# A fused attention and SiLU kernel: v's second cast and products moved ahead of q's last copies, batch 2's loads moved back, and the positions of the next two stages rewritten with them

## The chip, the cores and the metric

The kernel runs on one core of a Trainium2 chip. TensorE multiplies matrices into PSUM. VectorE and ScalarE read PSUM and write SBUF, [...]and SyncE (SP) issues most of the DMA transfers. The engines run beside each other, each in the order of its own list of instructions, and wait for one another through semaphores.

The metric is the device time of one execution, in microseconds (us). Before the change the median of four runs is 266.94 us (266.63 to 267.75).

## The reference

```python
def _attn_ref(q, k, v):                     # (8, 8, 576, 64): batch, head, row, d
    q_s = softmax(q, over d)
    k_s = softmax(k, over the 576 rows)
    kv = einsum('bhsd,bhse->bhde', k_s, v)
    return einsum('bhsd,bhde->bhse', q_s, kv)

def _moe_ref(x, w_in, w_out):               # x: (4608, 512)
    h = x @ w_in                            # (4608, 2048)
    return (h * sigmoid(h)) @ w_out         # (4608, 512)
```

The attention's output, heads side by side, is x. Inputs and output are float32 in memory; the products run on bfloat16.

## The kernel before

**Batches and stages.** There are eight batches (576 rows each) and nine stages t (512 rows of x each, except that stage 0 takes the whole first batch). Stage t computes the first layer for its rows (`mm1`, or `product1` where it uses Strassen's seven products for eight), SiLU (`act1`, `silu1`), and the second layer of the rows before it (`mm2` for stage 0, `product` and `after` for the others, the latter adding up the Strassen products and storing). The attention of batch b is prepared during stage b - 1, and `xt` makes the rows of x for stage t at the end of stage t - 1.

**One batch of attention**, in two halves `cc` of two head pairs each:

- `load` brings q, k and v from memory (`qt`, `kt`, `vt`; q and v have one buffer, k two).
- `exp` (ScalarE) makes `eq` and `ek`.
- `qsum` (VectorE) sums the rows of `eq`, `qnorm` scales them.
- `tr` and `trc` transpose `eq` on TensorE and copy the result to `qT`, each half in two pieces of 5 and 4 blocks; `tr_dma` lets the DMA engines do it instead.
- `vcast` casts v to `vaug`, which has a column of ones beside each head. `kv` (72 small products for a batch, 36 for a half) gives the score matrix and, from the column of ones, the divisor. `kvcopy` takes the reciprocal and scales to `kvn`.
- `xt` multiplies `kvn` and `qT`, `xtcopy` copies the result from PSUM to `XT`.

**PSUM.** `kv`, `tr`, `xt`, `mm1` and `product1` share a ring of six buffers; a product waits until the buffer that it is given has been copied or passed through SiLU. Two more buffers serve the second layer.

**Order.** The start (lines 598 to 646) is written out by hand for batch 0. `START['t']` says which engine makes each of the four transposed copies (0 VectorE, 1 GpSimd, 2 ScalarE), `START['h']` how many idle products `heat` puts at four places to keep TensorE busy. After that, everything is recorded with `put(t, position, function, ...)`, sorted by position and emitted: the tables `PLAN[t]`, `TXAT` and `TWAT` hold the positions. Within a stage the position counts TensorE's steps. So each engine's list follows from numbers, and an instruction only waits for what it needs and for what stands before it on its own engine.

The entries of `PLAN[t]` that matter here, for the batch prepared in stage t: `ex` positions of the four `exp` (q, q, k, k), `qs` and `qn` of `qsum` and `qnorm`, `vs` of `vcast`, `ks` and `kc` of `kv` and `kvcopy`, `ke` the engine of its scaling, `tp`, `tt`, `tc`, `te` of the transposes and their copies, `ox` and `oc` of `xt` and `xtcopy`, `lq`, `lk`, `lv` of the loads of the batch after. For the layers: `order` of the Strassen products (group, product), `sl` of the SiLUs, `add`, `act`, `s1` of the sums and SiLUs of those products, `xs` and `xe` of the four sums of XT (S1 to S4) that the products need, `pa`, `pb` and `pae` of `presum` (sums of the SiLU results), `y` and `ya` of the second layer's products and of `after`. `TXAT` and `TWAT` place the sums of the weights (`vsum` for the first layer, `wsum` for the second).

**Weights.** They come through GpSimd's queue, cast on the way, in the order of `WORDER`: w10 to w13, w20, q of batch 1, w21, w22, k, the first half of v, w23, the second half of v. `load_first` brings q, k and v of batch 2 on SP. It first lets VectorE write one element of the q buffer (line 663), so that the load waits for that point.

Of the kernel before, what the change touches and what calls it, by code (L numbers as in the profile page):

```python
# [18 lines left out]
PLAN = {  # L19
    0: {'y': [31.0, 33.0, 33.0, 33.5, 34.0, 34.5, 35.0, 35.5, 36.5, 37.0, 39.5, 41.5, 42.5, 44.5, 46.0, 47.0], 'ex': [31.7, 34.3, 39.3, 39.4], 'qs': [33, 35.5], 'qn': [37.0, 39.5], 'vs': [40.0, 37.5, 42.0, 43.5], 'ks': [45.0, 45.8], 'kc': [45.51, 46.31], 'lq': 39.0, 'tp': 39.0, 'ox': [47.1, 47.7], 'oc': [47.11, 47.71], 've': [1, 1, 1, 2], 'order': [(1, 0), (2, 0), (3, 1), (0, 1), (3, 0), (0, 0), (1, 1), (6, 0), (2, 1), (6, 1), (4, 0), (5, 0), (7, 1), (11, 0), (5, 1), (8, 1), (4, 1), (7, 0), (8, 0), (9, 0), (10, 1), (11, 1), (9, 1), (14, 0), (13, 1), (12, 1), (14, 1), (15, 0), (12, 0), (10, 0), (15, 1), (13, 0)], 'ke': [0, 1], 'oe': [0, 1], 'qe': [0, 0], 'pad': 16, 'th': [0, 1], 'tt': [43.5, 37.4, 42.0, 39.9], 'tc': [43.51, 41.5, 43.01, 41.0], 'te': [0, 2, 0, 2]},  # L20
    1: {'ex': [16.7, 16.72, 22.24, 23.26], 'qs': [17.65, 17.9], 'qn': [19.1, 18.1], 'vs': [22.5, 20.5], 'ks': [23.5, 25.5], 'kc': [26.01, 27.01], 'lq': 15.0, 'lk': 7.5, 'lv': 21.5, 'tp': 18.1, 'ox': [28.5, 29.0], 'oc': [29.01, 29.01], 've': [2, 2], 'pa': [10.9, 13.0, 15.0], 'pae': [0, 0, 0], 'ke': [0, 0], 'oe': [0, 2], 'std': 4, 'order': [], 'add': {}, 'act': {}, 's1': {0: 0, 1: 1, 2: 1, 3: 1}, 'sl': [0.5, 1.5, 3.5, 6.0, 6.0, 7.5, 7.0, 9.0, 9.0, 9.5, 11.5, 11.0, 14.5, 13.0, 15.0, 15.0], 'xs': [3.3, -24.9, -4.5, -2.5], 'xe': [1, 1, 0, 1], 'pad': 14, 'qe': [1, 0], 'th': [0], 'tt': [22.5, 21.1], 'tc': [23.51, 24.6], 'te': [2, 2]},
    2: {'std': 2, 'order': [(3, 1), (3, 6), (2, 1), (2, 6), (3, 7), (3, 5), (3, 2), (2, 7), (3, 4), (2, 2), (2, 5), (2, 4), (2, 3), (3, 3)], 'y': [-14.0, -12.5, -12.3, -12.25, -11.5, -11.0, -10.0, -9.5, -9.0, -5.0, -3.0, -2.5, -1.5, -0.5], 'ex': [0.2, -0.79, -3.6, -4.09], 'qs': [4.9, 3.4], 'qn': [11.91, 4.41], 'vs': [-3.08, 13.9], 'ks': [19.4, 20.9], 'kc': [19.91, 20.91], 'lq': 22.5, 'lk': 20.0, 'lv': 30.91, 'tp': 21.4, 'ox': [21.4, 21.4], 'oc': [21.41, 21.41], 'sl': [4.5, 8.5, 3.0, 5.5, 9.0, 9.0, 12.0, 10.5], 'add': {(3, 6): 9.55, (3, 3): 22.02, (3, 1): 9.55, (3, 5): 13.55, (3, 4): 17.55, (2, 2): 20.02, (3, 2): 20.02, (3, 7): 13.55, (2, 1): 10.55}, 'act': {(3, 5): 15.02, (3, 3): 22.02, (2, 5): 18.02, (3, 4): 19.02, (2, 4): 21.55, (2, 3): 22.02, (2, 7): 18.02, (3, 7): 14.55, (3, 2): 15.55, (2, 1): 12.02, (3, 6): 11.55}, 's1': {2: 0, 3: 0}, 'xs': [1.6, 2.6, 7.6, 4.6], 'pa': [18.95, 22.95, 20.95], 'ya': {2: -8.0, 6: -12.2, 3: 1.5, 5: -4.55}, 'm1': [1, 0], 'pb': [-14.9, -14.3, -12.39, -15.0, -5.0], 'xe': [0, 0, 0, 0], 'pae': [1, 0, 1], 'pbe': [0, 0, 0, 0, 0], 've': [1, 2], 'ke': [1, 0], 'oe': [1, 0], 'qe': [1, 1]},
}
# [4 lines left out]
PLAN[9] = {'y': [0, 1, 2, 3, 4, 5, 6, 7, 8, 9, 10, 11, 12, 13], 'ya': {}, 'm1': [0, 0], 'pb': [-0.201, -0.2, -0.2, 1.9, 2.9], 'pbe': [0, 0, 0, 0, 0]}  # L28
TXAT = [(0, (0, -5.5, 0, 0)), (0, (0, 20.0, 1, 1)), (1, (1, -28.5, 0, 0)), (1, (1, -6.0, 1, 1)), (2, (1, 2.0, 0, 0)), (2, (0, 12.5, 1, 0)), (3, (2, -23.5, 0, 0)), (3, (2, -30.5, 1, 1))]
TWAT = [(0, 26.0, 0), (1, 2.0, 0), (1, 2.0, 1), (1, 7.0, 1), (1, 12.5, 1), (0, 55.5, 0), (0, 32.0, 1), (0, 40.0, 0)]  # L30
WORDER = ['w10', 'w11', 'w12', 'w13', 'w20', 'q', 'w21', 'w22', 'k', 'v0', 'w23', 'v1']
# [3 lines left out]
STD = 0  # L35
START = {'qn': (0, 0), 'h': [4, 3, 2, 1], 'v': 0, 't': (0, 0, 0, 2), 'x': 1, 'o': 0, 'w': 4}

@with_exitstack
def kernel(
# [80 lines left out]
    def vcast(b, cc, eng, gs=(0, 2)):  # L120
        if gs[0] == gs[1]:
            return
        gs = slice(2 * cc + gs[0], 2 * cc + gs[1])
        o = vaug.rearrange("p j (g e) -> p j g e", e=E1)[:, :, gs, 0:D]
        i = st[b]["vt"][:, gs, :].rearrange("p g (j d) -> p j g d", d=D)
        if eng is nc.scalar:
            eng.copy(out=o, in_=i)
        else:
            eng.tensor_copy(o, i)
# [38 lines left out]
    def trc(b, cc, js, eng=nc.vector):  # L168
        t = st[b]["qtps", cc, js[0]]
        o, i = qt_tile(b)[:, cc, slice(*js), :], t[:, 0:js[1] - js[0], :]  # L170
        if eng is nc.scalar:
            eng.copy(out=o, in_=i)
        else:
            eng.tensor_copy(o, i)
# [16 lines left out]
    def kvcopy(b, cc, act=0):  # L191
        rzs = []
        for r in range(2):
            rz = ap.tile([128, 1], FP32, name="rz", bufs=4)
            nc.vector.reciprocal(out=rz, in_=st[b]["kvps", cc][r][:, D:E1])
            rzs.append(rz)
        for r in range(2):
            kp, rz = st[b]["kvps", cc][r], rzs[r]
            y = kvn[b % 3][:, cc, r, :]
            if act == 1 or act == 2 and r:  # L200
                nc.scalar.activation(out=y, in_=kp[:, 0:D], func=ACT.Copy, scale=rz[:, 0:1])
            else:
                nc.vector.tensor_scalar_mul(out=y, in0=kp[:, 0:D], scalar1=rz[:, 0:1])
# [29 lines left out]
    def xtcopy(t, cc, dve=0):  # L233
        for i, (off, size) in enumerate(part[t]):
            o1 = XO.pop((t, cc, i), None)
            if o1 is None:
                continue
            for g in range(2):
                x = XT[t][:, 2 * cc + g, off:off + size]
                if g < dve:  # L240
                    nc.vector.tensor_copy(x, o1[g][:, 0:size])  # L241
                else:
                    nc.scalar.copy(out=x, in_=o1[g][:, 0:size])  # L243
# [151 lines left out]
    ENG = (nc.vector, nc.gpsimd, nc.scalar)  # L395
# [198 lines left out]
    def heat(n):  # L594
        for _ in range(n):
            nc.tensor.matmul(out=wps, lhsT=warm[:, 0:128], rhs=warm, start=True, stop=True)

    HALF = ((0, 5), (5, J))
# [24 lines left out]
    for js in HALF:  # L623
        tr(0, 1, js)
    kvcopy(0, 0)
    for i, js in enumerate(HALF):
        trc(0, 1, js, ENG[SB["t"][2 + i]])
    heat(SB["h"][2])
    if SB["x"]:
        xt(0, 0)  # L630
    vcast(0, 1, nc.scalar, (0, 1))
    vcast(0, 1, ENG[SB["v"]], (1, 2))
    heat(SB["h"][3])
    kv(0, 1)
    if SB["x"]:
        xtcopy(0, 0, 1)
    kvcopy(0, 1, 2)
    if not SB["x"]:
        xt(0, 0)
        xtcopy(0, 0, 1)  # L640
    xt(0, 1)
# [143 lines left out]
```

The softmax here doesn't subtract the row's maximum and nothing guards it: scores larger than these inputs give would overflow.

## Time and profile before

| what | value |
|---|---|
| median of four runs | 266.94 us |
| the profiled execution | 267.75 us |
| its span on the core | 265.9 us |
| TensorE busy | 253.3 us |
| ScalarE busy | 188.0 us |
| VectorE busy | 196.2 us |
| GpSimd busy | 148.4 us |
| first product of `mm1` | 15.62 us |
| last product of stage 0's first layer | 31.3 us |
| first product of stage 1's first layer | 48.09 us |
| first product of stage 2's first layer | 75.24 us |
| first product of stage 3's first layer | 91.06 us |
| v's second half, batch 0: issued, landed | 3.34, 12.54 us |
| q, k, v of batch 2: issued on SP | 38.95, 39.42, 44.70 us |
| v of batch 3: issued, landed | 70.52, 78.02 us |

[...] The span runs from the first instruction to the last; the time holds 1.85 us more around it. Busy times of the other engines add up to much less than the span, and an idle stretch of theirs matters only if TensorE waits for what comes behind it.

### The profile page before, as it was taken

How to read it: one execution, taken by the hardware profiler on the slowest of the kernel's cores; microseconds unless marked ns; L12 is line 12 of the kernel's file. 1: busy time of each engine (PE TensorE's matmuls, PEld its weight loads, DVE VectorE, ACT ScalarE, POOL GpSimd, SP SyncE). 2: the span in 40 equal slices, each digit the busy share in tenths (PEclk: the TensorE clock that was granted, in tenths of full speed). 3: DMA queues.
4: the chain of work that ended last, by engine and by line, in shares of the span. 5: the costliest groups of instructions: out<-in, count | busy, mean ns of one | idle time of the engine just before them, and what ended most of it. 6: DMA issues, size and time to landing. Idle time of an engine off the chain costs nothing.

```text
span 265.9 us, 6578 instructions
## 1 busy us (share of the span) xinstructions
PE 253.3 (95%) x2690; PEld 200.4 (75%) x2695; DVE 196.2 (74%) x335; ACT 188.0 (71%) x326; POOL 148.4 (56%) x94
## 2 busy tenths in 40 slices
PE   8789999999999899999999989999999999999993
PEld 3468645457857688888888778888888887888882
DVE  2935185677887999689977598779877678898842
ACT  5689963869987899689968498879784557454300
POOL 2555047831128579757976785759676546603500
PEclk9999999999999999999999999999999999999999
DMA  7999999960998936757665756391621102110334
GB/s 253 324 206 270 231 333 396 359 202 8 222 300 237 297 121 198 149 160 282 208 130 151 293 184 128 85 346 48 141 73 41 39 22 59 42 39 12 76 75 118
DMA packets 39565, 45.61 MB, mean 172 GB/s; under 512 B 15216, under 2 KB 27504, under 8 KB 39536
## 3 DMA queue, kind: packets, MB, share of 16 engines
q1 hardware_dynamic: 34240, 37.33, 47.2%
q0 software_dynamic: 5136, 7.73, 13.2%
q8 instruction: 21, 0.34, 0.6%
q10 hardware_dynamic: 160, 0.13, 0.2%
q14 instruction: 8, 0.07, 0.1%
HBM read 36.70 MB, written 9.44 MB: 174 GB/s over the span
## 4 chain that ended last, share of the span: by engine, by line
PE 65%; DVE 14%; DMA 9%; ACT 3%; POOL 3%; issue 3%; SPq 1%; DVEq 0%; ACTq 0%; POOLq 0%
PE ops L450 24%; PE hps L349 19%; PE hps L256 13%; DMA kt<-in_k_dram 5%; PE ops L535 5%; DVE u L367 4%; DVE zq L137 3%; DMA qT<-eq 2%; PE kvps L183 2%; DMA qt<-in_q_dram 1%; PE o L225 1%; ACT eq L118 1%; SPq L524 1%; POOL eq L145 1%; DVE eq L145 1%
## 5 line engine op out<-in xcount | busy, mean ns | idle before, releaser
L450 PEld LDWEIGHTS <-GT 128*128 128x128 bf16 x512 | 49.6, 98 | 8.2 <-issue 2.0
L349 PEld LDWEIGHTS <-TX 128*128 128x128 bf16 x416 | 40.1, 98 | 8.6 <-issue 2.5
L349 PE MATMUL hps<-XS,TX 128*128 128x256 bf16 x312 | 43.3, 273 | 1.8 <-DVE XS L306 1.1
L367 DVE SCALAR_TENSOR_TENSOR u<-hps,s 128x512 f32<-128x512 f32 x52 | 35.4, 683 | 11.3 <-PE hps L349 9.2
L367 DVE SCALAR_TENSOR_TENSOR u<-hps,u 128x512 f32<-128x512 f32 x52 | 35.7, 687 | 10.6 <-PE hps L349 8.2
L450 PEld LDWEIGHTS <-SW 128*128 128x128 bf16 x384 | 37.2, 98 | 4.9 <-DVE SW L407 0.4
L391 ACT ACTIVATE GT<-u 128x512 bf16<-128x512 f32 x52 | 32.1, 631 | 7.5 <-DVE u L367 7.5
L256 PE MATMUL hps<-XT,W 128*128 128x320 bf16 (+3 forms) x223 | 35.4, 318 | 0.5 <-ACT XT L243 0.3
L349 PEld LDWEIGHTS <-W 128*128 128x128 bf16 x312 | 30.4, 98 | 4.4 <-issue 0.4
L450 PE MATMUL ops<-W,GT 128*128 128x256 bf16 x256 | 31.7, 273 | 1.4 <-ACT s L480 1.4
L450 PE MATMUL ops<-TW,SW 128*128 128x256 bf16 x256 | 32.9, 273 | 0.0
L450 PE MATMUL ops<-TW,GT 128*128 128x256 bf16 x256 | 32.6, 273 | 0.1
L256 PEld LDWEIGHTS <-W 128*128 128x128 bf16 x224 | 21.8, 98 | 13.3 <-issue 1.2
L137 DVE TENSOR_REDUCE zq<-eq 128x18 f32<-128x1152 bf16 x16 | 21.5, 1341 | 13.4 <-ACT eq L118 13.4
L349 PE MATMUL hps<-XT,W 128*128 128x256 bf16 x208 | 30.4, 273 | 0.4 <-DVE XT L241 0.4
L405 POOL TENSOR_TENSOR SW<-GT 128x1024 bf16<-128x1024 bf16 x7 | 14.9, 2128 | 27.9 <-ACT GT L391 17.4
L145 POOL TENSOR_TENSOR eq<-eq,rzq 128x1152 bf16<-128x1152 bf16 x11 | 23.6, 2151 | 10.8 <-DVE rzq L138 10.6
L411 POOL TENSOR_TENSOR SW<-GT,SW 128x1024 bf16<-128x1024 bf16 x11 | 23.6, 2146 | 9.1 <-DVE SW L407 9.1
L286 ACT ACTIVATE GT<-hps 128x192 bf16<-128x192 f32 (+4 forms) x72 | 25.3, 417 | 4.3 <-PE hps L256 2.9
L409 POOL TENSOR_TENSOR GT<-GT 128x1024 bf16<-128x1024 bf16 x12 | 25.5, 2128 | 0.1
L118 ACT ACTIVATE ek<-kt 128x1152 bf16<-128x1152 f32 x16 | 18.3, 1157 | 9.7 <-DMA kt<-in_k_dram 9.3
L391 ACT ACTIVATE GT<-s 128x512 bf16<-128x512 f32 x26 | 16.4, 632 | 10.1 <-DVE s L367 10.1
(81 smaller groups left out, 397.3 us busy)
## 6 DMA issues: line engine op xcount, KB each, us to landing
qt<-in_q_dram SPq DMA_DIRECT2D x6, 1152.0 KB, 5.7
kt<-in_k_dram SPq DMA_DIRECT2D x6, 1152.0 KB, 6.8
vt<-in_v_dram SPq DMA_DIRECT2D x6, 1152.0 KB, 8.2
out_dram<-u SPq DMA_DIRECT2D x34, 64.0 KB, 3.1
W<-in_moe_w_in_dram POOLq DMA_DIRECT2D x4, 512.0 KB, 8.7
W<-in_moe_w_out_dram POOLq DMA_DIRECT2D x4, 512.0 KB, 18.9
out_dram<-u SPq DMA_DIRECT2D x14, 128.0 KB, 2.6
qt<-in_q_dram SPq DMA_DIRECT2D x2, 576.0 KB, 4.1
```

Of the source, the lines that this page charges most:

```text
L118: nc.scalar.activation(out=o, in_=jgd(st[b][src], cc)[:, js], func=ACT.Exp)
L137: nc.vector.reduce_sum(out=st[b]["zq"][:, cc, js], in_=e, axis=AX.X)
L145: eng.tensor_tensor(out=e, in0=e, in1=r[:, :, :, None].to_broadcast([128, n, 2, D]), op=ALU.mult)
L256: nc.tensor.matmul(out=hps[:, 0:size], lhsT=W1[:, c, fb * 128:(fb + 1) * 128], rhs=XT[t][:, c, off:off + size], start=(c == 0), stop=(c == ...
L286: nc.scalar.activation(out=y, in_=hps[:, h], func=ACT.Silu)
L349: nc.tensor.matmul(out=o[:, f, :], lhsT=l(c, 2 * g + f), rhs=r(c), start=bool(first and f == 0 and c == 0), stop=(c == HK - 1), skip_group ...
L367: nc.vector.scalar_tensor_tensor(out=out, in0=o, scalar=1.0, in1=x, op0=ALU.mult, op1=ALU.add)
L391: nc.scalar.activation(out=y, in_=MP[t, g, x], func=ACT.Silu)
L405: V.tensor_add(S1[:, f], quad(t, 0, f, 1), quad(t, 1, f, 1))
L409: V.tensor_sub(quad(t, 0, f, 1), quad(t, 0, f, 0), quad(t, 0, f, 1))
L411: V.tensor_sub(S4[:, f], quad(t, 1, f, 0), S2[:, f])
L450: nc.tensor.matmul(out=o, lhsT=l(f), rhs=r(f), start=bool(first and (own or a == 0) and f == 0), stop=(f == HF - 1), skip_group_check=True,)
```

## The change

In the start, both parts of `vcast` for the second half of v, then `kvcopy(0, 0)`, `kv(0, 1)` and its `kvcopy` are emitted ahead of the last two transposed copies (`trc`) and of `xt(0, 0)`; the first of those copies goes from VectorE to ScalarE, and the switch `START['x']` is no longer read. The loads of batch 2 move from position 39.0 to 46.5. The positions of stages 1 and 2 and of the sums of the weights change in many places (of each table only the entries that change are shown, several to a line):

```diff
 PLAN[0]
-'lq': 39.0
+'lq': 46.5
 PLAN[1]
-'ex': [16.7, 16.72, 22.24, 23.26], 'qs': [17.65, 17.9], 'qn': [19.1, 18.1], 'vs': [22.5, 20.5]
+'ex': [15.2, 16.72, 23.24, 25.26], 'qs': [17.65, 20.4], 'qn': [23.1, 20.41], 'vs': [24.0, 17.5]
-'ks': [23.5, 25.5], 'kc': [26.01, 27.01], 'lk': 7.5, 'lv': 21.5, 'tp': 18.1
+'ks': [26.5, 26.5], 'kc': [26.51, 27.01], 'lk': 9.5, 'lv': 23.5, 'tp': 21.1
-'ox': [28.5, 29.0], 'oc': [29.01, 29.01], 'pa': [10.9, 13.0, 15.0], 'pae': [0, 0, 0]
+'ox': [28.5, 28.5], 'oc': [28.51, 29.51], 'pa': [10.9, 12.0, 12.0], 'pae': [0, 1, 0]
-'tt': [22.5, 21.1], 'tc': [23.51, 24.6], 'te': [2, 2]
+'tt': [23.5, 23.1], 'tc': [23.51, 27.61], 'te': [0, 2]
...
 PLAN[2]
-'order': [(3, 1), (3, 6), (2, 1), (2, 6), (3, 7), (3, 5), (3, 2), (2, 7), (3, 4), (2, 2), (2, 5), (2, 4), (2, 3), (3, 3)]
+'order': [(3, 1), (3, 6), (2, 1), (2, 6), (3, 5), (3, 7), (2, 2), (2, 7), (3, 2), (3, 4), (2, 5), (2, 4), (3, 3), (2, 3)]
-'y': [-14.0, -12.5, -12.3, -12.25, -11.5, -11.0, -10.0, -9.5, -9.0, -5.0, -3.0, -2.5, -1.5, -0.5]
+'y': [-14.0, -13.3, -12.5, -12.25, -11.5, -10.0, -9.5, -8.0, -6.0, -5.0, -3.0, -2.5, -1.5, -0.5]
-'ex': [0.2, -0.79, -3.6, -4.09], 'qs': [4.9, 3.4], 'qn': [11.91, 4.41], 'vs': [-3.08, 13.9]
+'ex': [0.2, 2.21, -2.1, -0.09], 'qs': [7.9, 6.9], 'qn': [14.91, 11.41], 'vs': [-2.08, 10.9]
-'ks': [19.4, 20.9], 'kc': [19.91, 20.91], 'lq': 22.5, 'lk': 20.0, 'lv': 30.91, 'tp': 21.4
+'ks': [19.4, 20.4], 'kc': [19.91, 20.41], 'lq': 20.5, 'lk': 19.5, 'lv': 24.91, 'tp': 19.9
-'ox': [21.4, 21.4], 'sl': [4.5, 8.5, 3.0, 5.5, 9.0, 9.0, 12.0, 10.5]
+'ox': [20.9, 20.9], 'sl': [2.5, 8.5, 3.0, 5.5, 10.5, 5.5, 11.5, 10.0]
-'s1': {2: 0, 3: 0}, 'xs': [1.6, 2.6, 7.6, 4.6], 'ke': [1, 0]
+'s1': {2: 0, 3: 1}, 'xs': [2.1, 4.1, 3.1, 6.6], 'ke': [1, 1]
...
-TXAT = [(0, (0, -5.5, 0, 0)), (0, (0, 20.0, 1, 1)), (1, (1, -28.5, 0, 0)), (1, (1, -6.0, 1, 1)), (2, (1, 2.0, 0, 0)), (2, (0, 12.5, 1, 0)), (3, (2, -23.5, 0, 0)), (3, (2, -30.5, 1, 1))]
+TXAT = [(0, (0, -8.0, 0, 0)), (0, (0, 20.5, 1, 1)), (1, (1, -29.0, 0, 1)), (1, (0, 24.5, 1, 0)), (2, (1, 0.5, 0, 0)), (2, (0, 9.0, 1, 0)), (3, (1, 2.0, 0, 0)), (3, (2, -29.5, 1, 1))]
-TWAT = [(0, 26.0, 0), (1, 2.0, 0), (1, 2.0, 1), (1, 7.0, 1), (1, 12.5, 1), (0, 55.5, 0), (0, 32.0, 1), (0, 40.0, 0)]
+TWAT = [(0, 30.0, 0), (0, 32.0, 1), (1, 4.0, 0), (1, 4.5, 1), (1, 13.5, 0), (0, 54.5, 0), (0, 32.5, 1), (1, 13.0, 0)]
...
-START = {'qn': (0, 0), 'h': [4, 3, 2, 1], 'v': 0, 't': (0, 0, 0, 2), 'x': 1, 'o': 0, 'w': 4}
+START = {'qn': (0, 0), 'h': [4, 3, 2, 1], 'v': 0, 't': (0, 0, 2, 2), 'x': 1, 'o': 0, 'w': 4}
...
     for js in HALF:
         tr(0, 1, js)
-    kvcopy(0, 0)
-    for i, js in enumerate(HALF):
-        trc(0, 1, js, ENG[SB["t"][2 + i]])
-    heat(SB["h"][2])
-    if SB["x"]:
-        xt(0, 0)
     vcast(0, 1, nc.scalar, (0, 1))
     vcast(0, 1, ENG[SB["v"]], (1, 2))
+    kvcopy(0, 0)
+    heat(SB["h"][2])
+    kv(0, 1)
+    trc(0, 1, HALF[0], ENG[SB["t"][2]])
+    kvcopy(0, 1, 2)
+    trc(0, 1, HALF[1], ENG[SB["t"][3]])
+    xt(0, 0)
     heat(SB["h"][3])
-    kv(0, 1)
-    if SB["x"]:
-        xtcopy(0, 0, 1)
-    kvcopy(0, 1, 2)
-    if not SB["x"]:
-        xt(0, 0)
-        xtcopy(0, 0, 1)
+    xtcopy(0, 0, 1)
     xt(0, 1)
```

Left out are the smaller shifts of the SiLUs and first sums of stage 1, of the single sums and SiLUs of stage 2 (`add`, `act`), and of `after`. As the lists of the engines come out: q, k and v of batch 2 stand on SP behind the stores of three of stage 0's four blocks of rows; v of batch 3 stands behind three stores of stage 1 instead of ahead of them; of the four exponentials of batch 3 one for k moves behind the copies of XT on ScalarE; on VectorE the four sums of XT in stage 2 stand ahead of batch 3's two row sums; the last product of stage 2 stands behind `xt` of stage 3 on TensorE. From stage 3's products on, the code is the same.

## The prediction

> **What bounds the kernel now.** I read the page first, then a table by stretches cut where TensorE's work changes, then TensorE's list of waits, and last the timelines of the engines in the two stretches that the change rebuilds. The page's line of busy time:
>
> ```profile
> PE 253.3 (95%) x2690; PEld 200.4 (75%) x2695; DVE 196.2 (74%) x335; ACT 188.0 (71%) x326; POOL 148.4 (56%) x94
> ```
>
> The table by stretches (from and to in us; length; busy us of PE, PEld, DVE, ACT, POOL; clock; DMA share; GB/s):
>
> ```profile
> 0.00:15.60 15.60, 12.08 (x139) 5.89 (x140) 10.01 (x23) 9.38 (x12) 7.69 (x17) 1.00 0.95 276
> 15.60:31.30 15.70, 15.70 (x131) 12.54 (x129) 5.80 (x6) 14.59 (x50) 4.93 (x5) 1.00 1.19 240
> 31.30:48.10 16.80, 16.22 (x162) 8.22 (x163) 9.61 (x19) 10.11 (x16) 9.39 (x7) 1.00 1.09 351
> 48.10:60.50 12.40, 12.31 (x64) 6.24 (x64) 8.75 (x9) 9.37 (x18) 6.50 (x3) 1.00 0.75 253
> 60.50:75.20 14.70, 14.63 (x210) 12.23 (x209) 12.04 (x24) 13.20 (x17) 2.12 (x1) 1.00 0.61 143
> 75.20:91.10 15.90, 15.20 (x178) 9.84 (x178) 13.76 (x27) 13.56 (x24) 9.92 (x5) 1.00 0.91 263
> ```
>
> From 15.6 us on TensorE is never idle for long, at full clock: the kernel ends when TensorE's list ends. A microsecond is won only where TensorE waits. Its waits (us in total, times, longest), and on TensorE's timeline (start, length) the largest place that the change can reach:
>
> ```profile
> PE ops L450 <- ACT s L480: 1.4, 1, 1.4
> ...
> PE hps L349 <- DVE XS L306: 1.1, 2, 0.6
> ...
> PE o L225 <- DVE kvn L203: 0.6, 1, 0.6
> ```
>
> ```profile
> 89.33 0.61 PE L349 MATMUL hps<-XS,W 128*128 128x256 bf16 x4
> 89.87 0.74 PE L225 MATMUL o<-qT,kvn 64*64 64x192 bf16 x16
> 91.06 0.60 PE L349 MATMUL hps<-XT,W 128*128 128x256 bf16 x4 [0.45 <-DVE XT L241]
> 91.49 1.04 PE L450 MATMUL ops<-W,GT 128*128 128x256 bf16 x8
> 93.11 0.61 PE L349 MATMUL hps<-XS,TX 128*128 128x256 bf16 x4 [0.58 <-DVE XS L306]
> ```
>
> Between the end of stage 2 and stage 3 TensorE stands 0.45 us for the copies of XT and 0.58 us for the sum S2 made from them. The 1.4 us wait lies at 153.7, in a stage whose code is unchanged. At the start, the first `mm1` waits behind `xt(0, 1)` (15.16), which waits for `kvn`.
>
> [...] stage 2's 32 matmuls of 512 columns run from 75.24 to 82.14, 0.2156 each, so 0.862 a block of four and 0.437 a Strassen product (0.109 x 4). [...] from 38 to 52 us both queues are at work and the table by 2 us shows 238 to 403 GB/s. [...] the same `wsum` takes VectorE 0.68 us alone and 2.59 at 53.78, beside GpSimd's.
>
> **The change, part by part.** Positions are read from the built order of each engine.
>
> *Start.* Both halves of v's second cast, `kv(0, 1)` and its copy now stand ahead of the last two transposed copies (now both on ScalarE) and of `xt(0, 0)`. The casts need v's second half, issued at 3.34 and landing 9.2 us later, at 12.54: VectorE is free at 12.34 and waits 0.2. ScalarE casts 12.58 to 13.26 (0.68, its row), VectorE to 13.24 (0.66 net of queueing). `kvn` of the first half comes to 13.87 (two reciprocals and two scalings, 0.63) where it was 12.93. `kv(0, 1)` runs 13.26 to 13.85, its `kvn` is ready at 14.45 where it was 15.16. But ScalarE makes the last transposed copy only then (14.4 to 14.98, 0.58), and the last pair of `xt(0, 1)` waits for a PSUM buffer that ScalarE's first XT copy frees at 15.28. So the first `mm1` starts at 15.43 instead of 15.62. Weight w10 landed at 14.96 and does not hold it. Gain 0.2.
>
> *Loads of batch 2, and the weight sums.* q, k and v leave SP after the stores of three token blocks, at about 48.1, instead of 38.95, 39.42 and 44.70. Three loads of 1152 KB at the 380 to 400 GB/s of that stretch take 9 us: q about 54, k 57, v 60. They are first used at 62.56, 66.5 and 64.7 (ScalarE). k of batch 3 follows on SP at 50.5 and is needed at 70. Cost 0, cover 4 us or more. The moved `vsum` and `wsum` (0.69 us each on VectorE, 2.13 on GpSimd) fall where both engines idle: before 34.5, and between 48 and 61.3. The last `presum` before the silus end must be done by 61.28; my sum gives 58.7, or 60.4 if one 2.1 us block by GpSimd falls on it. Cost 0.
>
> *End of stage 1.* The seventh product waits for `after` of the sixth as before (66.05); VectorE's order up to there is the same. Behind it the transposes and both `kv` are grouped, one change of tile shape less: 0.1 gained (68.67 to 69.27 is 0.60 for 9 transposes whose share is 0.50). v of batch 3 leaves SP behind three stores (1.8 us). It was issued at 70.52 but moved only after the transposes ended at 73.6, so I let it land at 78 to 79 (78.02 before). One exponential of k (1.11 us) moves from before to behind the XT copies on ScalarE, where it idled 0.75.
>
> *Stage 2.* ScalarE's first silu ends at 79.29 + 1.11 = 80.40; TensorE needs that buffer for its seventh block at 75.24 + 6 x 0.862 = 80.41. It just fits; the buffers after it have 0.3 or more to spare. VectorE does all four sums of XT before GpSimd starts (0.41 each instead of 0.97 and 0.78), then `qsum` twice: ready 80.2 and 81.7, so GpSimd's two `qnorm` end at 84.4 instead of 83.82 and the DMA transposes of batch 3, 4.6 us, land at 89.1 instead of 88.44. The 14 products (6.1 us) from 82.04 meet no new wait in my walk; `kv(3, 0)` at 87.4, `kv(3, 1)` at 88.4 after the sum of (2, 4), its copies on ScalarE 89.1 to 89.6, so `xt(3, ·)` runs 89.05 to 90.0, where it was 89.87 to 90.6. One product, (2, 3), now stands behind `xt`: TensorE works 90.0 to 90.45 while the copies run, and stage 3 begins at 90.45, not 91.06. S2 needs the last ScalarE copy (91.2) and two sums on VectorE (0.6, 0.42): the 93.11 product starts at 92.45. Gain over both steps 0.66, the 0.1 above in it.
>
> *Sum.* 0.2 + 0.66 = 0.86, taken as 0.9: 0.05 for two smaller shape changes that I did not follow. Behind it the order of every engine is the same and the chain of waits follows TensorE (each k load is issued behind stores that wait for products), so the gain stays. The profiled execution would go from 267.75 (span 265.9 and 1.85 around it) to 266.85. It is 0.81 above the median, 266.94: it holds the 1.45 wait at 153.69, whose k load took 8.46 us, while the next stage's (5.93 us) left none. Against the median: 266.0.
>
> **Bounds of what the trace doesn't show.** Start: from -0.2 (v late by 0.4, now with no slack; before the casts began 0.5 after landing) to 0.4 (both engines' copies without the buffer wait); taken 0.2. v of batch 3: 77.5 to 80.5, where 79.2 is the point from which it delays `qnorm`; a delay passes on one to one. The first silu: 0 to 0.4 of stall. Stage 2 to 3: gain from 0.1 to 1.0, the two waits together being 1.03.
>
> **Rivals.**
> *A. Half of it:* the start gives nothing, as v lands a little later and ScalarE's copies queue, and ScalarE's late silus or the transposes take 0.3 to 0.5 back. For: margins of 0.01 (the silu) and 0.0 (transposes 89.1 against 89.05). Against: only the first buffer is that tight, and `xt(3, ·)` begins with batch 2's columns, which need no transpose of batch 3. 266.94 - 0.3 = 266.6.
> *B. Slower, through v of batch 3:* its issue slips by 1.8 us to 72.3 or later, and if it again needs the 7.5 us of its row it lands near 80; with the output stores beside it, at 81 to 82. `vcast`, both `qnorm`, the transposes and `xt(3, ·)` then go late by 1.8 to 2.8; from 80.1 on the whole gain is gone. 266.94 - 0.9 + 1.9 = 267.9. Against: its first 3 us were spent behind the transposes, which the stores would use now.
> *C. No effect of the load move* is what I assume; if the early loads had held back w23 and v1 (landing 41.4 and 42.8), TensorE would show a wait for them, and it shows none.
>
> **How the numbers follow.** Main case 0.62 (own range 265.4 to 266.6), A 0.23, B 0.15. Predicted 266.0. The range 265.1 to 267.1 leaves out most of B and the main case's edge. A measurement of this kernel can tell about 0.3% (0.8 us) from no change: faster means under 266.14, slower over 267.74. The main case lies on that edge and is under it in three quarters of its chance: faster 0.48; same 0.37 (the rest of it, A and a little of B); slower 0.15 with what B holds and unseen stalls.
>
> **What would show it.** Start: first `mm1` at 15.3 to 15.5, VectorE's cast waiting for v. Loads: q of batch 2 issued near 48 and no ScalarE wait for it at 62. Stage 2: no TensorE wait on ScalarE's silus before 82; the transposes landing by 89.3. Stage 3: its first product at 90.2 to 90.6 and S2's at 92.2 to 92.7, both less the start's gain. It is wrong if `mm1` starts later than 15.6, if GpSimd's cast of v starts after 79.2, or if TensorE idles at 80 to 82.

## The result, and the profile after

The changed kernel takes 267.65 us in the median of 43 runs, the kernel before 266.89 in 64 runs beside it. The ratio is 1.0032, with a 95% interval from 1.0022 to 1.0042: slower by 0.3%, where 0.9 us less was predicted. In a second set of runs it is 1.0024 (1.0009 to 1.0040).

The page of the changed kernel (busy us, share of the span, number of operations by engine; then q14, one of the queues that the page labels `instruction`: packets, MB, share):

```profile
PE 254.1 (96%) x2689; PEld 200.7 (76%) x2695; DVE 191.9 (72%) x334; ACT 188.3 (71%) x327; POOL 147.8 (56%) x94
...
q14 instruction: 8, 0.07, 0.1%
```

VectorE has 334 operations and no longer 335; ScalarE has one more. This is the copy of q's transposes that the new start gives to ScalarE, and it will matter far from the start.

The profiled execution took 266.99 us (span 264.8), low among its own runs (266.72 to 270.29), while the one of before, 267.75, lay high among those of its kernel (265.80 to 268.11). Set side by side, the two pages show a gain where there is a loss; so the ledger below is made from places in the trace and from the medians, not from these two totals. The table by stretches, cut as before (length; busy us of PE, PEld, DVE, ACT, POOL; clock; DMA share; GB/s):

```profile
0.00:15.70 15.70, 12.29 (x138) 6.02 (x140) 9.99 (x23) 9.94 (x14) 7.58 (x17) 1.00 0.94 273
...
60.60:75.40 14.80, 14.73 (x210) 12.30 (x209) 12.46 (x26) 11.73 (x15) 2.12 (x1) 1.00 0.69 199
75.40:91.10 15.70, 15.51 (x177) 9.82 (x177) 12.95 (x25) 14.87 (x25) 9.80 (x6) 1.00 0.89 264
```

The stretch of stage 2 is 0.2 us shorter than before, the end of stage 1 0.1 longer, the start 0.1 longer. The head of the chain of waits (start, length, what):

```profile
3.35 9.34 DMA vt<-in_v_dram
12.69 0.02 issue
12.71 0.69 ACT vaug L127
13.40 0.04 issue
13.45 0.63 PE kvps L183 x32
...
15.15 0.64 PE o L225 x8
15.79 4.24 PE hps L256 x33
```

Before, the start hung on q's exponentials and their sums on VectorE; now it hangs on v's second load. From the beginning of the cast to the first `mm1` nothing has slack. TensorE's timeline at the end of stage 2 (start, length):

```profile
88.74 0.77 PE L183 MATMUL kvps<-vaug,ek 64*64 64x65 bf16 x36
89.45 1.28 PE L225 MATMUL o<-qT,kvn 64*64 64x192 bf16 x16
90.66 0.61 PE L349 MATMUL hps<-XS,W 128*128 128x256 bf16 x4
91.11 0.60 PE L349 MATMUL hps<-XT,W 128*128 128x256 bf16 x4
91.54 1.04 PE L450 MATMUL ops<-W,GT 128*128 128x256 bf16 x8
92.84 0.60 PE L349 MATMUL hps<-XS,TX 128*128 128x256 bf16 x4 [0.26 <-DVE XS L306]
```

The wait of 0.45 before stage 3 is gone and that for S2 is 0.26, not 0.58, but `xt` takes 1.28 us where it took 0.74 (a wait lies inside it, as told below, which the view shows as busy). S2's product is 0.27 earlier than before, 0.38 if counted from the first `mm1`.

All this gives a small gain. The loss sits where neither diff nor prediction had looked. VectorE's timeline in stage 7, in the changed kernel:

```profile
193.42 0.68 DVE L472 SCALAR_TENSOR_TENSOR s<-ops,s 128x512 f32<-128x512 f32 x1
194.63 0.69 DVE L367 SCALAR_TENSOR_TENSOR u<-hps,s 128x512 f32<-128x512 f32 x1 [0.53 <-PE hps L349]
195.78 0.69 DVE L367 SCALAR_TENSOR_TENSOR u<-hps,u 128x512 f32<-128x512 f32 x1 [0.46 <-DVE u L367]
196.38 0.68 DVE L367 SCALAR_TENSOR_TENSOR s<-hps,s 128x512 f32<-128x512 f32 x1
```

and the same operations in the kernel before:

```profile
194.82 0.68 DVE L472 SCALAR_TENSOR_TENSOR s<-ops,s 128x512 f32<-128x512 f32 x1
196.03 0.69 DVE L367 SCALAR_TENSOR_TENSOR u<-hps,s 128x512 f32<-128x512 f32 x1 [0.53 <-PE hps L349]
196.82 0.69 DVE L367 SCALAR_TENSOR_TENSOR u<-hps,u 128x512 f32<-128x512 f32 x1
197.77 0.69 DVE L367 SCALAR_TENSOR_TENSOR s<-hps,s 128x512 f32<-128x512 f32 x1 [0.26 <-PE hps L349]
```

Between the second and the third operation 0.79 us pass before, and 1.15 after. The third is said to wait for its own engine's last result, which is there at 195.32. The view of line 367 in this window, for the changed kernel (duration in ns, start):

```profile
L367 DVEq EVENT_SEMAPHORE  x1: 21/21/21, 195.4 to 195.4; - x1
...
L367 DVE SCALAR_TENSOR_TENSOR u<-hps,u x1: 692/692/692, 195.8 to 195.8; 128x512 f32<-128x512 f32 x1
```

The record of the wait (DVEq) lasts 21 ns and ends at 195.38, after the result is there, so I take the wait as met by then; yet the operation behind it begins only at 195.78, 0.40 after the end of the record. Before, the same pair stands at 196.8 and 196.82, and 0.04 lie between. VectorE pauses, for 0.36 us by the starts, without waiting for anything that the trace shows. TensorE needs the buffer that this operation reads:

```profile
195.74 0.60 PE L349 MATMUL hps<-XT,TX 128*128 128x256 bf16 x4
196.52 0.60 PE L349 MATMUL hps<-XS,W 128*128 128x256 bf16 x4 [0.18 <-DVE u L367]
```

From the first `xt` product for the rows of stage 7 (block 7) to that for stage 8 (block 8) it takes 25.46 us instead of 25.13. A second part lies outside the trace: a run's time less its span is 2.08 to 2.21 in all 44 runs of the changed kernel (median 2.14), and 1.81 to 1.92 in the runs of the kernel before (1.86).

### The profile page after: what moved, and what is told of

Read it like the earlier page. It is cut to its first block, busy times and chain, and to the rows that moved or that the text cites. A ratio compares the mean times of both kernels' runs of the same rounds, so it can differ in the third digit from the quotient of the medians.

```text
span 264.8 us, 6575 instructions
## 1 busy us (share of the span) xinstructions
PE 254.1 (96%) x2689; PEld 200.7 (76%) x2695; DVE 191.9 (72%) x334; ACT 188.3 (71%) x327; POOL 147.8 (56%) x94
## 4 chain that ended last, share of the span: by engine, by line
PE 73%; DVE 10%; DMA 9%; SPq 3%; ACT 2%; issue 2%; DVEq 0%; ACTq 0%
PE ops L450 28%; PE hps L349 23%; PE hps L256 13%; DMA vt<-in_v_dram 7%; PE ops L535 5%; DVE u L367 4%; DMA kt<-in_k_dram 2%; PE kvps L183 2%; PE o L225 2%; DVE zq L137 2%; SPq L524 1%; SPq L108 1%; DVE s L367 1%; ACT eq L118 1%; DVE u L472 1%
## 5 line engine op out<-in xcount | busy, mean ns | idle before, releaser
L407 POOL TENSOR_TENSOR SW<-SW,GT 128x1024 bf16<-128x1024 bf16 x8 | 17.5, 2188 | 11.3 <-DVE SW L405 10.8
```

The costliest lines, as they stand in the source:

```text
L407: V.tensor_sub(S2[:, f], S1[:, f], quad(t, 0, f, 0))
```

## The experiments

The first four take the change apart.

**The old start in the changed kernel**

```diff
-START = {..., 't': (0, 0, 2, 2), ...}
+START = {..., 't': (0, 0, 0, 2), ...}
+    kvcopy(0, 0)
+    for i, js in enumerate(HALF):
+        trc(0, 1, js, ENG[SB["t"][2 + i]])
+    heat(SB["h"][2])
+    xt(0, 0)
     vcast(0, 1, nc.scalar, (0, 1))
     vcast(0, 1, ENG[SB["v"]], (1, 2))
...
```

> The changed kernel with the start of the kernel before (kvcopy(0,0) and both copies of batch 0's second transposes ahead of v's second cast, START t = (0, 0, 0, 2)); the new place of batch 2's loads and the new tables of stages 1 and 2 stay. Theory S (v's second half has become the last thing that the start waits for, and its landing varies): the loss is all in the start, so this kernel gets back 0.8 and keeps what stages 2 and 3 gained, median 266.2 to 266.6, below the kernel before (ratio 0.997 to 0.999), first mm1 at 15.6. Theory P (the new tables of stages 1 and 2 lose the time): no better than the changed kernel, 267.3 to 267.7 (ratio 1.002 to 1.003). Theory L (batch 2's loads, issued at 48 and not at 39 to 45): also 267.3 to 267.7.

Measured: 266.17 us, ratio 0.9985 (0.9970 to 1.0001), first `mm1` at 15.51. The theory of the start (S) seemed to have it.

**The new start alone**

```diff
-START = {..., 't': (0, 0, 0, 2), ...}
+START = {..., 't': (0, 0, 2, 2), ...}
...
+    kv(0, 1)
+    trc(0, 1, HALF[0], ENG[SB["t"][2]])
+    kvcopy(0, 1, 2)
+    trc(0, 1, HALF[1], ENG[SB["t"][3]])
+    xt(0, 0)
...
```

> The kernel before with the new start alone. Theory S: the start alone makes it slower by 0.5 to 1.0, median 267.4 to 267.9 (ratio 1.002 to 1.004), with a long tail upward, first mm1 at 15.7 or later. Theories P and L: within 0.3 of the kernel before (first mm1 15.5 to 15.8).

Measured: 266.44, ratio 0.9996 (0.9981 to 1.0011), first `mm1` at 15.28. So the start alone doesn't cost the 0.5 to 1.0 that S asked for, and S falls as the cause of the loss.

**The loads alone**

```diff
 PLAN[0]
-'lq': 39.0
+'lq': 46.5
```

> The kernel before with batch 2's three loads put at place 46.5 of stage 0 and not at 39, nothing else. Theory L: slower by 0.5 to 0.8, and a wait for q, k or v of batch 2 or for a presum ends on TensorE between 48 and 75. Theories S and P: same as before within 0.2 (ratio 0.9995 to 1.0005), loads landing by 60 and used from 62.6.

Measured: 266.52, ratio 0.9998 (0.9974 to 1.0021); no new wait in its list. Its interval reaches up to 0.56 us, so the time alone would not exclude L; but a kernel further down is as slow without the move, and L falls.

**The tables alone**

The kernel before with `PLAN[1]`, `PLAN[2]`, `TXAT` and `TWAT` of the changed kernel:

```diff
 PLAN[1]
-'lk': 7.5, 'lv': 21.5, 'tp': 18.1
+'lk': 9.5, 'lv': 23.5, 'tp': 21.1
...
```

> The kernel before with the new tables of stages 1 and 2 (PLAN 1 and 2, TXAT, TWAT) alone; the start and the place of batch 2's loads stay. Theory P: slower by 0.5 to 0.8, ratio 1.002 to 1.003. Theory S: faster by 0.3 to 0.7 (ratio 0.9975 to 0.999), stage 3's first product 0.4 to 0.6 earlier after the first mm1 than before. Theory L: faster as well, since the loads are at their old place.

Measured: 266.43, ratio 0.9992 (0.9978 to 1.0007). None of the parts is slow, so P falls too; but this profile and that of the old start show a cost that those of the changed kernel do not. In the kernel with the old start SP issues v of batch 3 like this (start, length):

```profile
71.67 1.82 SPq L521 DMA_DIRECT2D out_dram<-c  x1
73.60 0.55 SPq L108 DMA_DIRECT2D vt<-in_v_dram  x1
...
85.72 2.79 SPq L159 DMA_TRANSPOSE qT<-eq  x1
```

GpSimd's cast of it:

```profile
80.39 1.16 POOL L129 CAST vaug<-vt 128x1152 bf16<-128x1152 f32 x1 [12.73 <-DMA vt<-in_v_dram]
```

and TensorE's `xt` products of stage 3:

```profile
89.09 0.48 PE L225 MATMUL o<-qT,kvn 64*64 64x192 bf16 x4
90.38 0.55 PE L225 MATMUL o<-qT,kvn 64*64 64x320 bf16 x12 [0.81 <-DMA qT<-eq]
```

That is the prediction's rival B: a store of c took 1.82 us on SP (0.65 in the changed kernel), v came behind it, and cast, `qnorm`, transposes and `xt` followed one another. Its price here is a wait of 0.81, 0.86 in the kernel with the tables alone; and both are still no slower than before.

The second four ran on one chip, to see which parts are slow only together.

**The changed kernel again**

> The changed kernel once more, next to the three below on one chip. Theory V (with the new tables v of batch 3 is issued on SP behind the three writes of c, 2 to 3 us later than before; the cast of v on GpSimd then holds up qnorm, the DMA transposes of q and the score product of batch 3, by an amount that varies with v's landing): 267.3 to 267.8 (ratio 1.002 to 1.004), GpSimd's cast of v after 79.3, a wait for the DMA transposes of 0.3 to 0.9 in the score product near 90. Theory I (start and tables are harmless alone, as measured, and cost only together): the same time, with TensorE slower somewhere than in the kernels with one part alone. Theory C (the first measurement's loss belongs to its chip): 266.0 to 266.6.

Measured: 267.60, ratio 1.0024 (1.0009 to 1.0040), with no long wait in `xt`. The loss came back beside a new set of runs of the kernel before, so C, which had 266.0 to 266.6, falls.

**v of batch 3 ahead of the stores of c**

```diff
 PLAN[1]
-'lv': 23.5
+'lv': 21.3
```

> The changed kernel with the load of v of batch 3 put back ahead of the writes of c on SP (PLAN 1, lv 23.5 to 21.3); nothing else differs on any engine. Theory V: issue near 70.6, GpSimd's cast of v at 78 to 79.2 (where it doesn't land late), transposes issued by 84, no wait for them in the score product of batch 3, first S2 product 10.2 to 10.5 after the first product of stage 2 (10.97 before; 11.5 where the wait was 0.8): faster than the changed kernel by 0.5 to 0.9. Theory I and theory C: the same as the changed kernel within 0.2.

Measured: 267.33, ratio 1.0005 (0.9990 to 1.0020), S2's product 10.50 after stage 2's first product, as in the changed kernel (10.49). v left SP at 70.90 and not at 72.62, but GpSimd's cast began only 0.4 us earlier (79.0 and 79.4). The median lies 0.27 under that of the changed kernel, with overlapping intervals.

**The changed kernel without the move of the loads**

```diff
 PLAN[0]
-'lq': 46.5
+'lq': 39.0
```

> The changed kernel with batch 2's loads back at place 39 (new start and new tables together, old loads). Theory I with the tables as the partner of the start: as slow as the changed kernel, ratio 1.002 to 1.004. Theory V: also as slow, since v of batch 3 is as late. Theory C: 0.998 to 1.000, the sum of the two parts measured alone (0.9996 and 0.9992). If the partner is the loads: 0.998 to 1.000 too, with the next kernel slow.

Measured: 268.13, ratio 1.0034 (1.0020 to 1.0049): as slow as the changed kernel, or slower.

**The changed kernel with the old tables**

The same four tables, back to those of the kernel before:

```diff
 PLAN[1]
-'lk': 9.5, 'lv': 23.5, 'tp': 21.1
+'lk': 7.5, 'lv': 21.5, 'tp': 18.1
...
```

> The changed kernel with the old tables of stages 1 and 2 (new start and new place of batch 2's loads alone). Theory V and theory C: 0.999 to 1.000 against before, as the parts alone (0.9996 and 0.9998). Theory I with the loads as the partner of the start: ratio 1.002 to 1.004, with TensorE waiting or slow between 16 and 62.

Measured: 266.87, ratio 1.0004 (0.9989 to 1.0019). Start and tables are harmless alone and slow together: I holds, with the tables as the start's partner. What do they share? Put side by side, all four kernels that hold both (the changed one twice, and the two variants of it) pause in stage 7 and have a time less span of 2.14 to 2.17 in the median; the other six, the kernel before among them, have neither. Counted in the compiled programs from 0, with semaphore waits and branches, VectorE's stream has 442 entries in those four, and 443 or 444 in the others: the start takes one copy from it, the tables one wait. In the 442 the met wait of stage 7 is entry 319 and the paused operation entry 320. So a new theory, F: a place in VectorE's instruction stream.

The other ten test it. In all of them the six DMA transposes, those of half of batch 2 and of batches 3 to 7, are left out: plain copies of the same bytes stand in their place, so the scores of these batches are those of untransposed q. They are compared with each other. VectorE's entries are those of the kernels with transposes.

```diff
-        eng.dma_start_transpose(out=o, in_=i)
+        eng.dma_start(out=o.rearrange("x a y -> x (a y)"), in_=i)
```

**The kernel before with copies**

> The kernel before with its six DMA transposes of q's exponentials replaced by plain copies of the same bytes in the same places of SP's queue, so the scores are those of untransposed q; VectorE's instruction stream keeps its 444 entries. It is the base for the three kernels below, which leave the same part out. All theories: 265.5 to 267, 25.12 from stage 7 to stage 8, time less span near 1.86.

**The changed kernel with copies**

> The changed kernel, transposes replaced by plain copies as in the first; VectorE's stream has 442 entries. Theory F (a place in the stream: VectorE pauses 0.35 in stage 7 where a wait is entry 319 and the operation after it entry 320, and the time outside the span is 0.3 longer with 442 entries): 25.46 from stage 7 to 8, time less span 2.14, median 0.3 to 0.7 above the first. Theory V (v of batch 3 lands late and the DMA transposes after it): the plain copies are shorter, so at most 0.2 above the first. Theory S (the start): 0.5 to 0.8 above, with neither sign.

**One more memset at the start of VectorE's stream**

```diff
     nc.vector.memset(vaug.rearrange("p j (g e) -> p (j g) e", e=E1)[:, :, D:E1], 1.0)
+    nc.vector.memset(vaug.rearrange("p j (g e) -> p (j g) e", e=E1)[:, :, D:E1], 1.0)
```

> The one above with VectorE's memset of vaug's ones done twice (88 ns at 2.9, where VectorE is idle until 5.6): 443 entries, and all that follows stands one place later. Theory F: the pause near 196 and TensorE's wait of 0.18 there are gone, 25.12 from stage 7 to 8, time less span 1.75 to 1.85, median 0.5 to 0.7 below the one above and not above the first. Theories V and S: the same as the one above within 0.2.

**One more memset at its end**

```diff
         last_add(q, a)
+        if a == 0:
+            nc.vector.memset(warm[0:1, 0:1], 0.0)
```

> The changed kernel with copies for transposes and one more VectorE memset of one element at its end, between the last two pairs of additions: 443 entries as well, but everything before stands where it stood. Theory F: the pause stays (25.46), while time less span goes to 1.75 to 1.85 if it hangs on the number of entries; median 0.3 below the changed kernel with copies. If the time outside hangs on what stands in stage 7, 2.14 stays. Theories V and S: no change.

**Two instructions fewer in the kernel before**

```diff
-    nc.vector.memset(dummy, 0.0)
+    nc.gpsimd.memset(dummy, 0.0)
-    nc.vector.tensor_copy(ident, ident_f)
+    nc.gpsimd.tensor_copy(ident, ident_f)
```

> The kernel before (transposes replaced by plain copies as in the others of this kind) with two of VectorE's set-up instructions given to GpSimd, the memset of dummy and the cast of the identity: VectorE's stream has 442 entries and not 444, nothing else moves. Theory F: the pause of 0.35 near 195 and 25.46 from stage 7 to 8 appear in the kernel before, and time less span goes from 1.85 to 2.1 to 2.2; median 0.5 to 0.7 above the kernel before with copies. Were both effects tied to the change itself (its start or its tables) they would stay away: 25.12 and 1.85.

The table has all kernels: VectorE's entries; from block 7's first `xt` product to block 8's; time less span (median); median time; ratio to the kernel before, whose time stood at 266.65 to 267.12 beside the experiments.

| kernel | entries | block 7 to 8 | less span | us | ratio |
|---|---|---|---|---|---|
| before | 444 | 25.13 | 1.86 | 266.89 | 1 |
| changed | 442 | 25.46 | 2.14 | 267.65 | 1.0032 |
| changed, again | 442 | 25.46 | 2.17 | 267.60 | 1.0024 |
| changed, v early | 442 | 25.46 | 2.15 | 267.33 | 1.0005 |
| changed, old place of loads | 442 | 25.48 | 2.16 | 268.13 | 1.0034 |
| changed, old start | 443 | 25.13 | 1.81 | 266.17 | 0.9985 |
| changed, old tables | 443 | 25.12 | 1.83 | 266.87 | 1.0004 |
| before, new start | 443 | 25.12 | 1.77 | 266.44 | 0.9996 |
| before, loads | 444 | 25.12 | 1.90 | 266.52 | 0.9998 |
| before, tables | 443 | 25.12 | 1.79 | 266.43 | 0.9992 |
| copies: before | 444 | 25.12 | 1.85 | 265.89 | 0.9960 |
| copies: changed | 442 | 25.47 | 2.16 | 265.99 | 0.9962 |
| copies: changed, memset first | 443 | 25.12 | 1.81 | 265.53 | 0.9938 |
| copies: changed, memset last | 443 | 25.47 | 1.83 | 265.97 | 0.9956 |
| copies: before, two fewer | 442 | 25.46 | 2.16 | 266.51 | 0.9989 |
| copies: changed, old start | 443 | 25.12 | 1.83 | 265.28 | 0.9935 |
| copies: before, new start | 443 | 25.12 | 1.79 | 265.81 | 0.9958 |
| copies: changed, v early, memset first | 443 | 25.13 | 1.83 | 265.60 | 0.9947 |
| copies: before, 62 more | 506 | 25.13 | 1.80 | 265.76 | 0.9951 |
| copies: before, 30 more | 474 | 25.13 | 1.78 | 266.26 | 0.9978 |

One memset of 88 ns, done where VectorE is idle, removes the pause. VectorE's timeline with it:

```profile
194.14 0.69 DVE L367 SCALAR_TENSOR_TENSOR u<-hps,s 128x512 f32<-128x512 f32 x1 [0.53 <-PE hps L349]
194.94 0.69 DVE L367 SCALAR_TENSOR_TENSOR u<-hps,u 128x512 f32<-128x512 f32 x1
195.89 0.69 DVE L367 SCALAR_TENSOR_TENSOR s<-hps,s 128x512 f32<-128x512 f32 x1 [0.26 <-PE hps L349]
```

and taking two entries out of the kernel before, which has neither the start nor the tables, brings it:

```profile
193.77 0.69 DVE L367 SCALAR_TENSOR_TENSOR u<-hps,s 128x512 f32<-128x512 f32 x1 [0.53 <-PE hps L349]
194.91 0.69 DVE L367 SCALAR_TENSOR_TENSOR u<-hps,u 128x512 f32<-128x512 f32 x1 [0.46 <-DVE u L367]
195.52 0.68 DVE L367 SCALAR_TENSOR_TENSOR s<-hps,s 128x512 f32<-128x512 f32 x1
```

That kernel's median is 0.62 above the one it was made from (266.51 and 265.89; 0.34 of pause and 0.31 outside make 0.65), although the two were timed in different sessions. The memset at the end parts the two effects, as expected: the entries up to stage 9 stand where they stood and the pause stays (194.63, idle 0.45), while time less span falls to 1.83. The pause belongs to a place, the time outside to the number of entries or to what stands last. The median did not follow here: 265.97, and 265.99 without that memset, where 0.3 less was expected; each has an interval of 0.4 us to either side.

In medians the memset first is worth 0.46 us against the changed kernel with copies (265.53 and 265.99), with overlapping intervals (0.9915 to 0.9960, and 0.9947 to 0.9977); the shift of the two places is seen in each kernel's profile and in disjoint values of time less span. One expectation failed: the changed kernel with copies is 0.10 above the kernel before with copies (265.99 and 265.89), not 0.3 to 0.7. It has the pause and the longer time outside; but with copies the change also gains more from the first `mm1` to S2's product, 0.59 and not 0.38, as told below.

**What the start is worth, free of the pause**

The edits are those of the first two experiments, with copies for transposes.

> The changed kernel with copies for transposes and the start of the kernel before (443 entries, free of the pause): against the changed kernel with the memset done twice it differs in the start alone. Theory S: first mm1 at 15.5 to 15.7, not tied to v's landing, where the new start has it 3.02 after the cast of v's second half begins (15.3 to 16.2); median 0.1 to 0.3 lower than with the new start. As the prediction had it (the new start gains 0.2): 0.2 higher.

> The kernel before with copies for transposes and the new start alone (443 entries, free of the pause). Theory S: first mm1 at 15.3 to 16.2, 3.02 after the cast of v's second half begins; everything after mm1 as in the kernel before with copies (77.5 from the first mm1 to S2's product); median 0 to 0.3 above that kernel. As the prediction had it: 0.2 below.

Over all profiles the first `mm1` starts at 15.46 to 15.73 with the old start (nine, mean 15.61) and at 15.28 to 16.19 with the new one (eleven, mean 15.79). With the new start it comes 3.01 or 3.02 us after ScalarE's cast of v's second half begins, every time; the cast began anywhere between 12.27 and 13.17. The medians differ by 0.25 on the new tables (265.28 and 265.53) and not on the old (265.81 and 265.89), within what the timing can tell. So the new start is 0.18 later in the mean of the profiles, with a spread of 0.9 that leaves the size uncertain, and the times do not tell.

**v early, free of the pause**

The changed kernel with copies, the memset done twice at the start, and

```diff
 PLAN[1]
-'lv': 23.5
+'lv': 21.3
```

> The changed kernel with copies for transposes, with v of batch 3 loaded ahead of the writes of c (lv 21.3) and the memset done twice (443 entries). Theory F: no pause, 25.12, 1.75 to 1.85. Theory V: with the short copies v's place matters little, 76.9 to 77.1 from the first mm1 to S2's product as in the changed kernel with copies (76.9), median within 0.2 of the changed kernel with copies and the memset twice.

Measured: 265.60; GpSimd's cast of v at 77.19 (79.10 without the early load), and the same 76.89 from the first `mm1` to S2's product. With the copies, which SP issues in 0.49 to 0.51 us where a transpose takes it 1.40 to 3.25, v's place doesn't matter.

**Which places**

The kernel before with copies and 62 memsets of one element (30 in the other):

```diff
+    for _ in range(62):
+        put(0, 10.0, V.memset, dummy, 0.0)
```

> The kernel before with copies for transposes and 62 memsets of one element on VectorE in stage 0, where it is idle (at about 20): the stream has 506 entries, 64 more than the 442 of the kernels that pause, and the wait and the addition of stage 7 stand at 383 and 384. Theory F with a step of 64 entries: the pause of 0.35 and 25.46 from stage 7 to 8 are back, time less span 2.1 to 2.2 if that hangs on the number modulo 64. With a step of 128 (192 and 320 are the places seen): no pause, 25.12. If what counts is that the stream is short (442): no pause and 1.85.

> The same with 30 memsets: 474 entries, 32 more than 442, the wait and the addition at 351 and 352. Theory F with a step of 64: no pause there, 25.12 from stage 7 to 8, time less span 1.75 to 1.9. With a step of 32 or 16: the pause and 25.46 are back.

The pair of stage 7 runs through in both, at entries 383 and 384, or 351 and 352. But with 30 more VectorE pauses elsewhere, in stage 6 and before another operation (`issue` means that the profile shows no wait):

```profile
178.82 0.27 DVE L138 RECIPROCAL rzq<-zq 128x18 f32<-128x18 f32 x1
179.45 0.69 DVE L472 SCALAR_TENSOR_TENSOR u<-ops,s 128x512 f32<-128x512 f32 x1 [0.36 <-issue]
```

and TensorE waits for it:

```profile
180.19 1.03 PE L450 MATMUL ops<-TW,GT 128*128 128x256 bf16 x8 [0.35 <-DVE u L472]
```

Counted along the trace, this operation is entry 320 and stands behind a met wait at 319, with 0.40 between them: the pause stays at its place and takes whatever operation comes to stand there. In the kernel with 62 more no wait is entry 191 or 319, and it does not pause. The two were timed side by side: 266.26 and 265.76 (ratios 0.9978, 0.9961 to 0.9996, and 0.9951, 0.9936 to 0.9965), the one with the pause 0.50 slower, with time less span the same.

The second place is 192, with 0.40 or 0.41 between the met wait and the operation. The seven kernels that pause in stage 7 pause there too (near 130 us), and so do the three with 444 entries, the kernel before among them. (With 30 more such a pair stands at 191 and 192 too, but there the operation before it is still running.) In those three another operation is entry 192, and the view puts its idle time down to TensorE:

```profile
130.03 0.69 DVE L367 SCALAR_TENSOR_TENSOR u<-hps,s 128x512 f32<-128x512 f32 x1 [0.42 <-PE hps L349]
```

In none of these ten does TensorE wait there for VectorE. Pairs at 255 and 256 (in the kernels with 443 entries), at 351 and 352 and at 383 and 384 run through with 0.04 to 0.05. So steps of 32 and 64 entries are out, and the two places seen lie 128 entries apart.

The best kernel with its transposes is the changed one with the old start, 0.9985 (0.9970 to 1.0001), which is not told apart from the kernel before. The changed kernel with the memset and with its transposes has not been measured.

## Why the prediction was wrong

*Start.* Predicted 0.2 gained, with the lower bound "v late". Measured 0.18 lost in the mean, and the sign that `mm1` starts later than 15.6 came true. Two terms were off. v's second half was put at 12.54, from one profile, so that ScalarE's cast would begin at 12.58. In the mean it landed at 12.61 in the nine profiles with the old start and at 12.76 in the eleven with the new one, where the cast began at 12.78; whether the new start or chance makes that difference is not shown. And 2.85 us from the cast to the first `mm1` (12.58 to 15.43) are 3.02, which alone leaves next to nothing of the 0.2. As said, the last pair of `xt(0, 1)` waits for ScalarE's first copy of XT: it ends 2.75 after the cast begins (2.70 said), but the first `mm1` comes 0.27 behind it, and not 0.15. The shape was right: VectorE's cast waits for v.

*Loads of batch 2.* Right: moved alone they change nothing (0.9998), q is issued at 48.29, and ScalarE's list of waits is empty from 60 to 66.

*End of stage 1.* Predicted 0.1 gained. From the first `mm1` to stage 2's first it is 59.62 before, 59.71 after, and 59.49 with copies for transposes: gained only where no DMA transpose is in the way. In the changed kernel the one of batch 2 took 5.1 us and not 4.6, landed at 74.23 and not at 73.64, and held up `xt` of block 2, which takes 0.80 and not 0.63. The prediction put no wait on this transpose.

*Stage 2.* The first silu just fits, as said: TensorE has no wait before 82. `qnorm` ended at 84.7 (84.4 predicted), and the DMA transpose of batch 3 took 4.7 us (4.6) and landed at 89.4 (89.1). `xt` of stage 3 began at 89.45 and did not wait for it: rival A's margin of nothing held. What stretched `xt` to 1.28 is the second half of `kvn`, which ScalarE made from 89.75 and not from 89.1 to 89.6, since `kv(3, 1)` had waited until 88.99 for the buffer that VectorE's sum frees. In the changed kernel with copies, which land at 87.99, it is the same (ScalarE, then TensorE):

```profile
89.28 0.52 ACT L201 ACTIVATE kvn<-kvps,rz 128x64 bf16<-128x64 f32 x2 [0.15 <-DVE rz L195]
```

```profile
88.97 1.28 PE L225 MATMUL o<-qT,kvn 64*64 64x192 bf16 x16
```

Stage 3's first product came at 91.11 (90.2 to 90.6 said). From stage 2's first product to S2's it is 17.87 before, 17.40 after and 17.42 with copies, so 0.45 to 0.47 gained where 0.56 was said. (The terms that the prediction gives for S2, 91.2, 0.6 and 0.42, make 92.22; it took 92.45.) With the end of stage 1, from the first `mm1` to S2's product, the gain is 0.38 with transposes and 0.59 with copies (77.49, then 77.11 and 76.90), against 0.66.

*v of batch 3.* SP's stores were right. The cast began after 79.2, one of the signs of being wrong: at 79.37, 79.54 and 80.04 in the kernels with new start and new tables, 80.39 and 80.62 with the old start. Rival B's price was seen, 0.81 and 0.86, but in two kernels that are not slow.

*Sum.* Here it failed, and with it the sign of the change. "Behind it the order of every engine is the same and the chain of waits follows TensorE ... so the gain stays": the order was the same, the places were not. Two entries fewer on VectorE put an operation of stage 7 on a place at which the engine pauses (0.34 lost) and lengthen the time around the span (0.3 lost in the median). The prediction had taken the time around the span as a constant 1.85, and gave no rival to it. Without these two the change would have gained 0.20, not 0.86, by the sizes above.

The ledger: 0.38 gained from `mm1` to S2, less 0.18, 0.34 and 0.3, is 0.44 slower. Measured were 0.76 and, in the second set of runs, 0.50 in the medians (0.64 by the ratio). With copies the same sum is 0.23 slower, and 0.10 was measured. What is left, up to 0.3, is not settled. Between the first `xt` products of blocks 4 and 7, where the code is unchanged, the ten profiles with transposes differ by up to 1.7 us, so single profiles can't place it. Late transposes in some of the runs would give it (the kernel with v early is 0.27 faster), but no profile of the changed kernel caught such a run.

## What to carry to other kernels

Compare time less span as well as the span: a difference there that no run of the other kernel reaches isn't made by the waits in the trace. When parts are harmless alone and slow together, look for what they add up to, here the number of entries in one engine's stream, and test it with a single idle instruction before any deeper story. Then look at that place in the profiles of all the other kernels too, whatever operation stands there: here that showed a second place, 192, and that no step of 32 or 64 entries fits. And one profile of each kernel can show the opposite sign of the medians; a load that loses its slack should be priced with the spread of its landing, not with one value.

## What the runs showed that was not expected

VectorE paused for some 0.36 us between a met wait and the next operation where that operation is entry 192 or 320 of its stream, and not at 256, 322, 352 or 384. Near the pause at 320 stands a packet of q14, 8,192 bytes by the trace. In the changed kernel one comes right behind the pause (the view of DMA from 196.3 to 196.8):

```profile
q14 instruction: 1, 0.01, 5.0%
```

In all eight profiles with a pause at entry 320 such a packet starts 0.67 to 0.74 us after the operation begins. In eleven of the other twelve it comes at 188.7 to 192.4, when VectorE has begun no entry later than 316; in the twelfth, with 62 more, VectorE is busy then. And the kernels with 474 and 506 entries have nine of these packets within the span, all others eight:

```profile
q14 instruction: 9, 0.07, 0.1%
```

The packet comes after the pause, so VectorE does not stand for it. What VectorE does in that time, why it pauses at these two entries, and what the packets have to do with it was not shown.

The time around the span was 2.14 to 2.17 us with 442 entries on VectorE and 1.77 to 1.90 with 443, 444, 474 or 506. Nothing in the trace lies there, so its cause stays open.

Plain copies in place of six DMA transposes brought the kernel before from 267.12 to 265.89 us (0.9960, 0.9944 to 0.9976), although the first 93 us show no difference (77.49 from the first `mm1` to S2's product in both). It lies further on: from block 4's first `xt` product to block 6's it is 53.2 to 54.7 us in the ten profiles with transposes and 52.1 to 53.1 in the ten with copies (means 53.64 and 52.51). Which wait makes it was not followed.
